# Shifting attention scores bank by bank in a fused attention and feed-forward kernel, with value products and the first unit's work re-slotted

## Chip, cores, metric

One Trainium2 chip, one core. The metric is device time in microseconds for one execution, as a median over runs.

TensorE, VectorE, ScalarE and GpSimd are called PE, DVE, ACT and POOL, as in the profile; PEld is PE's weight load. The clock in a profile is the share of PE's full clock that was granted.

## The reference

Pooled attention for 8 batches of 8 heads (sequence 576, head size 64; keys and values averaged over 8 rows, so 72 keys), then a feed-forward layer with a snake activation, all in float32:

```python
scores = scale * np.matmul(q, k_p.transpose(0, 1, 3, 2))        # (8, 8, 576, 72)
scores = scores - np.max(scores, axis=-1, keepdims=True)        # "the shift"
attn = np.exp(scores); attn = attn / (np.sum(attn, -1, keepdims=True) + 1e-09)
x = attention_output(attn, v_p)          # (4608, 512)
h = x @ w_in                             # (4608, 2048)
s = np.sin(alpha * h)
g = h + s * s / (alpha + 1e-09)
out = g @ w_out                          # (4608, 512)
```

## The kernel before

The hidden layer runs as nine units of 512 tokens. A unit is 28 slots, four groups of seven products (a Strassen scheme); a slot is four matmuls of 128x128x256, 1.73 us of PE. The attention for the next unit's tokens is slipped between slots. So unit 0 holds the attention of batch 1 (and the rest of batch 0), units 1 to 6 that of batches 2 to 7, and units 7 and 8 have none. The output layer follows.

A `slot` first runs what is left of the slot before, then the extra attention work, then its product:

```python
for slot in range(7 * self.NJ):
    J, k = divmod(slot, 7)
    for f in self.left: f()          # bank-to-bank copies and sines (ACT), sums (DVE)
    for f in extra[slot]: f()        # attention work
    ...                              # k == 0: b1 = bank(); left0: b6 = bank(); k == 1: b5 = bank(); left2: b7 = bank()
    product(p, ...)                  # p = (1, 5, 6, 2, 7, 3, 4)[k]
```

The kernel uses PSUM as eight banks. Banks 0 to 4 rotate (`bank()` takes the next), 5 to 7 serve attention. Scores come in pairs of tiles, two banks a tile: banks 5 and 6, and banks x and 7, where x is the rotating bank that the next group will take. A shift is two DVE instructions (maximum, subtract) over both banks at once:

```python
def two_scores(j):
    x = (self.turn + 1) % 5
    views = []
    for i, (c, d) in ((2 * j, (5, 6)), (2 * j + 1, (x, 7))):
        m = 6 if i == 3 else NP
        ps = self.PS[:, c:d + 1:d - c, 0:m * Sp].rearrange("p e (h k) -> p e h k", h=m)   # banks c and d
        ...                                                # score matmuls into ps
    for i, m, ps in views[::-1 if j else 1]:
        mx = self.sm.tile([P, 2, 6], F32, name="mx2")
        nc.vector.tensor_reduce(out=mx[:, :, 0:m], in_=ps, axis=AX, op=OP.max)
        nc.vector.tensor_tensor(out=E(i)..., in0=ps, in1=mx..., op=OP.subtract)
```

The products with the values use half or a quarter of PE's rows each. `halves` are products on 64 rows, `last_keys` on 32; `ordered` is a tiny DVE copy that keeps products on different rows apart when they write one bank (`rest`). Here hp = 0, 1 use rows 0-63 and hp = 2, 3 rows 64-127:

```python
halves(ps[2], main[2], True); halves(rest[:, 0], ...); halves(rest[:, 1], ...)
ordered()
for hp in (0, 1): halves(ps[hp], main[hp], True)
halves(rest[:, 2], ...); halves(rest[:, 3], ...)
halves(ps[3], main[3], True)
for hp in (0, 1): last_keys(rest[:, hp], more[hp])
ordered()
for hp in (0, 2, 1, 3): last_keys(ps[hp], main[hp])
for hp in (2, 3): last_keys(rest[:, hp], more[hp])
```

Of the kernel before, what the change touches and what calls it, by code (L numbers as in the profile page):

```python
# [13 lines left out]
F32 = mybir.dt.float32  # L14
AX = mybir.AxisListType.X
AF = mybir.ActivationFunctionType
OP = mybir.AluOpType
PSUM = bass.MemoryType.PSUM

P = 128  # L20
# [20 lines left out]
class Kernel:  # L41
    def __init__(self, tc, q, k, v, w_in, w_out, alpha, out):
        self.tc, self.nc = tc, tc.nc
        self.q, self.k, self.v = q, k, v
        self.w_in, self.w_out, self.alpha, self.out = w_in, w_out, alpha, out
        self.B, self.H, self.S, self.D = q.shape
        self.Sp = self.S // POOL
        self.DM = self.H * self.D
        self.FF = w_in.shape[1]
        self.K1 = self.DM // P  # L50
        self.K2 = self.FF // P
        self.NP = self.H // 2
        self.NU = self.B * self.S // (2 * TH)
        self.NJ = self.K2 // 2 // JW
        self.xT = {}
        self.T = self.S // 4

        self.gd = self.nc.dram_tensor("g_bridge", (2, self.NJ * JW, P, self.B * self.S), F32, kind="Internal").ap()
# [154 lines left out]
    def attention(self, b):  # L213
# [19 lines left out]
                nc.tensor.transpose(ps[:, j, :], kp[:, j].rearrange("p e d -> p (e d)"), self.ident[:NP * m, :NP * m])  # L233
            nc.vector.tensor_copy(out=kb[:].rearrange("p hp (x j) -> p j hp x", j=3), in_=ps.rearrange("p j (hp x) -> p j hp x", hp=NP))

        def q_t(i):

            n = rows[i]
            x = self.qm[b][:n].rearrange("p (t hp x) -> p t hp x", t=5, hp=NP)[:, i]
            if b not in self.qt:  # L240
                self.qt[b] = self.qt_view(self.qp.tile([P, 5 * H * D], F32, name="q"))
            ps = self.abank([P, NP, P])
            for hp in range(NP):
                nc.tensor.transpose(ps[:, hp, :n], x[:, hp], self.ident[:n, :n])
            nc.scalar.copy(out=self.qt_tiles(b)[:, i, :, :n], in_=ps[:, :, :n])

        def columns(hp, i):

            if b < 2:
                return [(c, self.qt_tiles(b)[:, i, hp, c:c + 64]) for c in range(0, rows[i], 64)]  # L250
            if i < 4:
                return [(64 * c, self.qt[b][:, i, hp, 2 * c:2 * c + 2].rearrange("p t i -> p (t i)")) for c in range(2)]
            return [(32 * a, self.qt[b][:, a, hp, 4]) for a in range(2)]

        def two_scores(j):

            x = (self.turn + 1) % 5
            views = []
            for i, (c, d) in ((2 * j, (5, 6)), (2 * j + 1, (x, 7))):
                m = 6 if i == 3 else NP  # L260
                ps = self.PS[:, c:d + 1:d - c, 0:m * Sp].rearrange("p e (h k) -> p e h k", h=m)
                views.append((i, m, ps))
                for t in (i, 4) if i == 3 else (i,):
                    for hp in range(NP):
                        r0, h = (64 * (hp // 2), NP + hp % 2) if t == 4 else (0, hp)
                        for r, q in columns(hp, t):
                            for e in range(2):
                                s = slice(64 * e, 64 * e + 64)
                                nc.tensor.matmul(ps[r0 + r:r0 + r + q.shape[-1], e, h, :], q[s], kb[s, hp, :], start=True, stop=True)  # L269
            for i, m, ps in views[::-1 if j else 1]:  # L270
                mx = self.sm.tile([P, 2, 6], F32, name="mx2")
                nc.vector.tensor_reduce(out=mx[:, :, 0:m], in_=ps, axis=AX, op=OP.max)  # L272
                nc.vector.tensor_tensor(out=E(i).rearrange("p (e h) k -> p e h k", e=2), in0=ps,  # L273
                                        in1=mx[:, :, 0:m].unsqueeze(3).to_broadcast([P, 2, m, Sp]), op=OP.subtract)

        def products(i):

# [226 lines left out]
        def all_values():  # L504

            hps = 0, 2, 1, 3
            ps = dict(zip(hps, (self.psum([P, 4 * P], i) for i in (5, 6, 7, (self.turn + 4) % 5))))
            rest = self.psum([P, 4, 64], (self.turn + 1) % 5)
            main, more = ({hp: value_parts(hp, r) for hp in hps} for r in (False, True))

            def halves(o, parts, start):
                for e, (w, x) in enumerate(parts[0]):
                    nc.tensor.matmul(o[64 * e:64 * e + 64], w, x, start=start, stop=False, skip_group_check=True)  # L513

            def last_keys(o, parts):
                w, x = parts[1]
                nc.tensor.matmul(o, w.rearrange("p e d -> p (e d)"), x, start=False, stop=True, skip_group_check=True)  # L517
            def ordered():
                nc.vector.tensor_copy(out=self.sm.tile([P, 1], F32, name="order")[:], in_=rest[:, 1, 0:1])
            halves(ps[2], main[2], True)  # L520
            halves(rest[:, 0], more[0], True)
            halves(rest[:, 1], more[1], False)
            ordered()
            for hp in (0, 1):
                halves(ps[hp], main[hp], True)
            halves(rest[:, 2], more[2], False)
            halves(rest[:, 3], more[3], False)
            halves(ps[3], main[3], True)
            for o, hp in ((rest[:, 0], 0), (rest[:, 1], 1)):
                last_keys(o, more[hp])  # L530
            ordered()
            for hp in hps:
                last_keys(ps[hp], main[hp])
            for hp in (2, 3):
                last_keys(rest[:, hp], more[hp])
            self.vp.pop(b)
            for hp in hps:
                to_x(ps[hp].rearrange("p (t j) -> p j t", t=4), hp, 0, 512)
            to_x(rest, slice(0, 4), 512, 64)

        return SimpleNamespace(**{f.__name__: f for f in (k_t, q_t, products, score, two_scores, exp, norm, new_a, turn, move, values, values_rest, all_values,
                                                          k_head, q_head, rest_q, products_head, soft_head, norm_head, norm_rest, a_head, a_rest)})


# [261 lines left out]
    def first_batch(self):  # L806

        nc = self.nc
# [44 lines left out]
                A.norm_head(hp - 1, nc.vector if hp == 1 else nc.gpsimd)  # L853
        self.load_q_rest(0, self.q_rest)
        self.load_q(1)
        self.load_w_in_part(1)
        for e in range(2):
            self.load_k(1, e)
        A.norm_head(3, nc.vector)
        self.sum_v_rows(0, 0, 2)  # L860
        A.a_head(0, (1, 7, 0))
# [8 lines left out]
    def carry(self, u):  # L870
# [5 lines left out]
        if u == 0:  # L876
            A0, A = self.att[:2]
            at(1, A0.values, (2, 3), (2, 7))
            at(1, self.sums_of_x, 0, 1)
            at(1, self.sums_of_x, 0, 2)  # L880
            at(1, self.sums_of_x, 0, 3)
            at(2, self.load_w_in_part, 2)
            at(2, self.load_w_in_part, 3)
            at(3, A0.rest_q)
            at(3, A0.score, 4)
            at(3, self.pairs_q, 1, (0, 1))
            at(4, self.pairs_q, 1, (2, 3, 4))
            at(5, self.combine_w_in, 1, (0, 1))
            at(6, self.combine_w_in, 1, (2, 3))
            at(6, A.k_t)  # L890
            at(7, self.load_v, 1, 0)
            at(7, self.load_v, 1, 1)
            for i in range(5):
                at((4, 5, 6, 7, 8)[i], A.q_t, i)
            for i in range(2):
                at((10, 12)[i], A.two_scores, i)
            for i in range(4):
                at((14, 15, 15, 15)[i], A.exp, i)
                at((15, 15, 16, 16)[i], A.norm, i)
                at((16, 16, 17, 17)[i], A.turn, i)  # L900
            at(10, self.combine_w_in, 2, (0, 1, 2, 3), self.nc.gpsimd)
            at(16, self.combine_w_in, 3, (0, 1, 2, 3), self.nc.gpsimd)
            at(15, A0.exp, 4)
            at(20, A0.norm_rest)
            at(23, A0.a_rest)
            at(24, lambda: A0.values_rest((5, 6, 7, (self.turn + 1) % 5)))
            at(17, A.new_a)
            at(17, A.move, 0)
            at(17, A.move, 1)
            at(25, A.all_values)  # L910
            at(9, self.load_q, 2)
            at(14, self.load_q, 3)
            for e in range(2):
                at(16, self.load_k, 2, e)
            at(26, self.att[2].k_t)
            turn = 23
        else:
            at(0, self.sums_of_x, u, 2)
            at(0, self.sums_of_x, u, 3)
        if 0 < u < last:  # L920
            A = self.att[b]
            for i in range(2):
                at((3, 5)[i], A.two_scores, i)
            for i in range(4):
                at((8, 9, 10, 10)[i], A.exp, i)
                at((9, 10, 11, 11)[i], A.norm, i)
                at((12, 12, 13, 13)[i], A.turn, i)
# [335 lines left out]
```

## Time and profile before

| | before |
|---|---|
| time, median (lowest to highest) | 975.57 us (972.2 to 980.65, 4 runs) |
| profiled span | 969.3 us |
| PE busy, whole span | 920.7 us, 95% |
| PE idle from slot 1 of unit 0 (27.9 us) to the value products of unit 6 | 37.5 us |
| time at half clock in that stretch | 23.9 us (seven windows of 3.41 us) |
| output stage | 368 us at full PE, not touched |

How to read it: PE is the bound, so the question is where PE stands still and where its clock is halved. The lines for that are in the prediction: shares, waits of PE, the sums by unit, and the chain of unit 1. (The chain is the work that ended last, followed back from each piece to what released it.) The numbers in `name <- name: 26.7, 10, 2.9` are microseconds in total, how many waits, and the longest. Lines of source are named L721 and so on; L269 is the score matmul, L272 and L273 the shift, L721 the products of the hidden layer, L700 and L788 DVE's sums, L513 and L517 the 64-row and 32-row value products.

### The profile page before, as it was taken

What the parts mean: (1) busy time and instruction counts of PE and PEld (TensorE: products, weight loads), DVE (VectorE), ACT (ScalarE), POOL (GpSimd) and SP (SyncE); (2) the same over time, 40 slices, a digit from 0 to 9 for tenths busy, and PEclk for the clock granted to TensorE, in tenths of its full rate; (3) what the DMA queues carried; (4) which work ended last, traced back from release to release, by engine and by line L of the source; (5) the groups of instructions that cost most, each with busy time, mean ns of one, the idle gap of its engine ahead of it and who ended that gap; (6) DMA issues with size and microseconds to landing.
All of it is one profiled execution on the core that took longest, in us unless ns stands there. A gap on an engine that the chain in (4) does not pass through costs nothing.

```text
span 969.3 us, 17586 instructions
## 1 busy us (share of the span) xinstructions
PE 920.7 (95%) x6953; PEld 828.6 (85%) x6953; DVE 667.7 (69%) x990; ACT 434.4 (45%) x995; POOL 154.1 (16%) x147
## 2 busy tenths in 40 slices
PE   7977899998997998989999999999999999999997
PEld 6766678886786876878888889999999999999997
DVE  6548574664645654647346688997979797979795
ACT  3745576674763864757688662111111111111111
POOL 4257151341412503412000000000000000000000
PEclk9999999999998998999999999999999999999999
DMA  9964656666565563661642724625253625252511
GB/s 245 229 190 119 177 154 174 196 166 185 148 175 164 142 173 99 173 191 58 225 170 87 234 88 122 203 75 172 74 172 74 172 74 172 77 171 75 173 23 37
DMA packets 134130, 141.12 MB, mean 146 GB/s; under 512 B 49808, under 2 KB 102048, under 8 KB 134048
## 3 DMA queue, kind: packets, MB, share of 16 engines
q1 hardware_dynamic: 132976, 138.81, 49.5%
q10 hardware_dynamic: 1072, 1.19, 0.4%
q8 instruction: 55, 0.90, 0.4%
q14 instruction: 27, 0.22, 0.1%
HBM read 75.37 MB, written 47.19 MB: 126 GB/s over the span
## 4 chain that ended last, share of the span: by engine, by line
PE 83%; DVE 7%; ACT 4%; issue 1%; POOL 0%; DMA 0%; SPq 0%; DVEq 0%; ACTq 0%
PE PS L1019 39%; PE PS L721 39%; PE PS L513 2%; DVE mx L272 2%; DVE ex L273 2%; ACT s L734 2%; DVE h L788 1%; PE PS L269 1%; PE PS L517 1%; DVE sm L305 1%; DVE h L700 1%; ACT s L727 1%; ACT PS L747 0%; ACT ex L299 0%; ACT p L761 0%
## 5 line engine op out<-in xcount | busy, mean ns | idle before, releaser
L721 PE MATMUL PS<-home,a 128*128 128x256 f32 x1152 | 274.8, 391 | 25.3 <-DVE ex L273 17.1
L721 PEld LDWEIGHTS PS<-home,a 128*128 128x128 f32 x1152 | 222.8, 196 | 62.7 <-DVE ex L273 18.0
L721 PE MATMUL PS<-home,as 128*128 128x256 f32 x864 | 203.2, 384 | 10.5 <-DVE ex L273 9.6
L721 PEld LDWEIGHTS PS<-home,as 128*128 128x128 f32 x864 | 163.4, 191 | 35.8 <-DVE ex L273 10.3
L1019 PE MATMUL PS<-s,wb 128*128 128x144 f32 x896 | 119.4, 286 | 0.4 <-ACT PS L1132 0.4
L700 DVE TENSOR_TENSOR h<-PS,p 128x512 f32<-128x512 f32 x72 | 49.2, 684 | 98.2 <-PE PS L721 56.6
L1019 PEld LDWEIGHTS PS<-s,wb 128*128 128x128 f32 x896 | 113.7, 190 | 0.7 <-ACT PS L1132 0.6
L734 ACT ACTIVATE s<-s,c 128x256 f32<-128x256 f32 (+1 forms) x216 | 110.0, 572 | 0.0
L117 POOL TENSOR_TENSOR kvin<-kvin 96x768 f32<-96x768 f32 (+3 forms) x42 | 70.1, 1669 | 205.1 <-DMA kvin<-in_v_dram 186.3
L727 ACT ACTIVATE s<-h,al 128x256 f32<-128x256 f32 x144 | 65.2, 501 | 78.1 <-DVE h L700 78.1
L727 ACT ACTIVATE s<-PS,al 128x256 f32<-128x256 f32 x144 | 60.0, 467 | 54.2 <-PE PS L721 42.4
L1132 ACT COPY PS<-PS 128x144 f32<-128x144 f32 x56 | 14.7, 263 | 146.0 <-PE PS L1019 144.6
L788 DVE TENSOR_TENSOR h<-PS,s 128x512 f32<-128x512 f32 x36 | 24.6, 684 | 73.1 <-ACT s L734 73.1
L1019 PE MATMUL PS<-r,wb 128*128 128x144 f32 x512 | 73.2, 286 | 0.0
L1019 PE MATMUL PS<-s,a 128*128 128x144 f32 x512 | 73.2, 286 | 0.0
L1019 PEld LDWEIGHTS PS<-r,wb 128*128 128x128 f32 x512 | 67.1, 190 | 0.1
L1019 PEld LDWEIGHTS PS<-s,a 128*128 128x128 f32 x512 | 67.0, 190 | 0.0
L1019 PE MATMUL PS<-s,we 128*128 128x144 f32 x384 | 54.9, 286 | 0.0
L1019 PE MATMUL PS<-x,wb 128*128 128x144 f32 x384 | 54.9, 286 | 0.0
L1151 ACT COPY PS<-PS 128x144 f32<-128x144 f32 x56 | 14.7, 263 | 88.2 <-PE PS L1019 88.2
L1019 PEld LDWEIGHTS PS<-s,we 128*128 128x128 f32 x384 | 50.4, 190 | 0.1
L1019 PEld LDWEIGHTS PS<-x,wb 128*128 128x128 f32 x384 | 50.3, 190 | 0.0
(176 smaller groups left out, 1175.4 us busy)
## 6 DMA issues: line engine op xcount, KB each, us to landing
g_bridge<-h SPq DMA_DIRECT2D x72, 512.0 KB
r<-g_bridge SPq DMA_DIRECT2D x31, 1152.0 KB
out_dram<-o SPq DMA_DIRECT2D x128, 72.0 KB
kvin<-in_k_dram SPq DMA_DIRECT2D x14, 576.0 KB
q<-in_q_dram SPq DMA_DIRECT2D x7, 1024.0 KB
kvin<-in_v_dram SPq DMA_DIRECT2D x14, 512.0 KB
aM<-tr SPq DMA_DIRECT2D x56, 92.0 KB
aM<-tr SPq DMA_DIRECT2D x56, 88.0 KB
```

Of the source, the lines that this page charges most:

```text
L117: self.nc.gpsimd.tensor_tensor(out=t[..., 0:w] if w > D else out, in0=t[..., 0:w], in1=t[..., w:2 * w], op=OP.add)
L272: nc.vector.tensor_reduce(out=mx[:, :, 0:m], in_=ps, axis=AX, op=OP.max)
L273: nc.vector.tensor_tensor(out=E(i).rearrange("p (e h) k -> p e h k", e=2), in0=ps, in1=mx[:, :, 0:m].unsqueeze(3).to_broadcast([P, 2, m, S ...
L513: nc.tensor.matmul(o[64 * e:64 * e + 64], w, x, start=start, stop=False, skip_group_check=True)
L700: add = lambda o, x, y: nc.vector.tensor_tensor(out=o, in0=x, in1=y, op=OP.add)
L721: nc.tensor.matmul(ps[:, jj, :], self.A[p][:, kk, f * P:(f + 1) * P], x[:, kk, :], start=(start and jj == 0 and kk == 0), stop=(kk == 1), ...
L727: nc.scalar.activation(out=G.s[:, i, jj, j, :], in_=src[:, jj], func=AF.Sin, scale=self.al[:, f:f + 1])
L734: nc.scalar.activation(out=x, in_=x, func=AF.Square, scale=self.c[:, f:f + 1])
L788: add = lambda o, x, y: self.nc.vector.tensor_tensor(out=o, in0=x, in1=y, op=OP.add)
L1019: nc.tensor.matmul(out, W[:, J // 2, J % 2, :], A[:, J, :], start=(start and J == 0), stop=(J == self.NJ - 1), skip_group_check=True)
L1132: nc.scalar.copy(out=x1[:, 0, :], in_=x0[:, 1, :])
L1151: nc.scalar.copy(out=x1[:, 1, :], in_=x1[:, 0, :])
```

## The change

The intent: take PE's waits for the shift away, spread DVE's work over more slots, place value products so that row halves alternate, and unbunch the attention work of unit 0. The diff, cut to its core:

```diff
-            for i, (c, d) in ((2 * j, (5, 6)), (2 * j + 1, (x, 7))):
+            for i, banks in ((2 * j, (x, 7)), (2 * j + 1, (5, 6))):
-                ps = self.PS[:, c:d + 1:d - c, 0:m * Sp].rearrange(...)
+                ps = [self.psum([P, m, Sp], c) for c in banks]
-            for i, m, ps in views[::-1 if j else 1]:   (both shifts at once)
+            for i, m, ps in tiles:
+                self.shifts.append(lambda i=i, m=m, ps=ps: shifts(i, m, ps))
+            two_shifts()
+            if j == 0:
+                two_shifts()
+        def shifts(i, m, ps):            # odd tiles: one view of banks 5:7; even tiles: bank by bank
+            if i % 2: ps, y = [self.PS[:, 5:7, 0:m * Sp]...], [y]
+            else:     y = y[:, 0], y[:, 1]
+            for z, o in zip(ps, y): (reduce max of z, then o = z - max)
 # value products
-            for hp in (0, 1):
+            for hp in (0, 3, 1):
                 halves(ps[hp], main[hp], True)
 ...
-            halves(ps[3], main[3], True)
-            last_keys of rest 0, 1
+            last_keys of ps[2], ps[3], then of rest 0, 1
             ordered()
-            last_keys of ps[0], ps[2], ps[1], ps[3]
+            last_keys of ps[0], ps[1]
             last_keys of rest 2, 3
 # units 1 to 6
+            at(6, A.two_shifts)          # the last shift, one slot after its scores (slot 5)
 # unit 0 (slots, before -> after)
 #   keys of batch 1 loaded before, not after, the second part of w_in
 #   rest_q 3 -> 2; k_t 6 -> 4; q_t 4,5,6,7,8 -> 4,4,7,8,9 (the first two copied by DVE, not ACT)
 #   pairs_q(2, 3, 4): slot 4 in both, but now behind q_t and k_t in program order
 #   two_scores 10, 12 -> 5, 10 with the last shift at 11; exp 14,15,15,15 -> 9,9,15,15
 #   norm 15,15,16,16 -> 10,10,16,16; turn 16,16,17,17 -> 13,13,17,17
 #   w_in sums of part 1: DVE, slots 5, 6 -> POOL, slot 4; of part 3: POOL, slot 16 -> 10
```

More of the change, by code (lines that the diff above doesn't have):

```diff
@@ L54, in __init__ @@
         self.NJ = self.K2 // 2 // JW
-        self.xT = {}
+        self.xT, self.shifts = {}, []
         self.T = self.S // 4
@@ L234, in k_t, with q_t @@
             nc.vector.tensor_copy(out=kb[:].rearrange("p hp (x j) -> p j hp x", j=3), in_=ps.rearrange("p j (hp x) -> p j hp x", hp=NP))
-        def q_t(i):
+        def q_t(i, copy=nc.scalar.copy):
             n = rows[i]
@@ L244, in q_t @@
                 nc.tensor.transpose(ps[:, hp, :n], x[:, hp], self.ident[:n, :n])
-            nc.scalar.copy(out=self.qt_tiles(b)[:, i, :, :n], in_=ps[:, :, :n])
+            copy(out=self.qt_tiles(b)[:, i, :, :n], in_=ps[:, :, :n])
         def columns(hp, i):
             if b < 2:
+                if i == 4:
+                    return [(0, self.qt_tiles(b)[:, 4, hp, 0:64])]
                 return [(c, self.qt_tiles(b)[:, i, hp, c:c + 64]) for c in range(0, rows[i], 64)]
@@ L257, in two_scores @@
             x = (self.turn + 1) % 5
-            views = []
-            for i, (c, d) in ((2 * j, (5, 6)), (2 * j + 1, (x, 7))):
+            tiles = []
+            for i, banks in ((2 * j, (x, 7)), (2 * j + 1, (5, 6))):
                 m = 6 if i == 3 else NP
-                ps = self.PS[:, c:d + 1:d - c, 0:m * Sp].rearrange("p e (h k) -> p e h k", h=m)
-                views.append((i, m, ps))
+                ps = [self.psum([P, m, Sp], c) for c in banks]
+                tiles.append((i, m, ps))
                 for t in (i, 4) if i == 3 else (i,):
@@ L268, in two_scores, with two_shifts @@
                                 s = slice(64 * e, 64 * e + 64)
-                                nc.tensor.matmul(ps[r0 + r:r0 + r + q.shape[-1], e, h, :], q[s], kb[s, hp, :], start=True, stop=True)
-            for i, m, ps in views[::-1 if j else 1]:
-                mx = self.sm.tile([P, 2, 6], F32, name="mx2")
-                nc.vector.tensor_reduce(out=mx[:, :, 0:m], in_=ps, axis=AX, op=OP.max)
-                nc.vector.tensor_tensor(out=E(i).rearrange("p (e h) k -> p e h k", e=2), in0=ps,
-                                        in1=mx[:, :, 0:m].unsqueeze(3).to_broadcast([P, 2, m, Sp]), op=OP.subtract)
+                                nc.tensor.matmul(ps[e][r0 + r:r0 + r + q.shape[-1], h, :], q[s], kb[s, hp, :], start=True, stop=True)
+            for i, m, ps in tiles:
[3 more added lines that the diff above has]
+                two_shifts()
+        def two_shifts():
+            self.shifts.pop(0)()
+        def shifts(i, m, ps):
+            y = E(i).rearrange("p (e h) k -> p e h k", e=2)
+            if i % 2:
+                ps, y = [self.PS[:, 5:7, 0:m * Sp].rearrange("p e (h k) -> p e h k", h=m)], [y]
+            else:
+                y = y[:, 0], y[:, 1]
+            for z, o in zip(ps, y):
+                w = list(z.shape)[:-1]
+                mx = self.sm.tile([P, 12], F32, name="mx2")[:, 0:m * (1 + i % 2)]
+                if i % 2:
+                    mx = mx.rearrange("p (e h) -> p e h", e=2)
+                nc.vector.tensor_reduce(out=mx, in_=z, axis=AX, op=OP.max)
+                nc.vector.tensor_tensor(out=o, in0=z, in1=mx.unsqueeze(len(w)).to_broadcast(w + [Sp]), op=OP.subtract)
         def products(i):
@@ L527, in all_values @@
             halves(rest[:, 3], more[3], False)
-            halves(ps[3], main[3], True)
-            for o, hp in ((rest[:, 0], 0), (rest[:, 1], 1)):
-                last_keys(o, more[hp])
+            for hp in (2, 3):
+                last_keys(ps[hp], main[hp])
+            for hp in (0, 1):
+                last_keys(rest[:, hp], more[hp])
             ordered()
-            for hp in hps:
+            for hp in (0, 1):
                 last_keys(ps[hp], main[hp])
@@ L539, in all_values @@
             to_x(rest, slice(0, 4), 512, 64)
-        return SimpleNamespace(**{f.__name__: f for f in (k_t, q_t, products, score, two_scores, exp, norm, new_a, turn, move, values, values_rest, all_values,
+        return SimpleNamespace(**{f.__name__: f for f in (k_t, q_t, products, score, two_scores, two_shifts, exp, norm, new_a, turn, move, values, values_rest, all_values,
                                                           k_head, q_head, rest_q, products_head, soft_head, norm_head, norm_rest, a_head, a_rest)})
@@ L855, in first_batch @@
         self.load_q(1)
-        self.load_w_in_part(1)
         for e in range(2):
             self.load_k(1, e)
+        self.load_w_in_part(1)
         A.norm_head(3, nc.vector)
@@ L883, in carry @@
             at(2, self.load_w_in_part, 3)
-            at(3, A0.rest_q)
+            at(2, A0.rest_q)
             at(3, A0.score, 4)
             at(3, self.pairs_q, 1, (0, 1))
+            at(4, self.combine_w_in, 1, (0, 1, 2, 3), self.nc.gpsimd)
+            at(4, A.q_t, 0, self.nc.vector.tensor_copy)
+            at(4, A.q_t, 1, self.nc.vector.tensor_copy)
+            at(4, A.k_t)
             at(4, self.pairs_q, 1, (2, 3, 4))
-            at(5, self.combine_w_in, 1, (0, 1))
-            at(6, self.combine_w_in, 1, (2, 3))
-            at(6, A.k_t)
             at(7, self.load_v, 1, 0)
             at(7, self.load_v, 1, 1)
-            for i in range(5):
-                at((4, 5, 6, 7, 8)[i], A.q_t, i)
             for i in range(2):
-                at((10, 12)[i], A.two_scores, i)
+                at((5, 10)[i], A.two_scores, i)
+            at(11, A.two_shifts)
+            for i in range(2, 5):
+                at(5 + i, A.q_t, i)
+            at(9, A0.exp, 4)
             for i in range(4):
-                at((14, 15, 15, 15)[i], A.exp, i)
-                at((15, 15, 16, 16)[i], A.norm, i)
-                at((16, 16, 17, 17)[i], A.turn, i)
+                at((9, 9, 15, 15)[i], A.exp, i)
+                at((10, 10, 16, 16)[i], A.norm, i)
+                at((13, 13, 17, 17)[i], A.turn, i)
             at(10, self.combine_w_in, 2, (0, 1, 2, 3), self.nc.gpsimd)
-            at(16, self.combine_w_in, 3, (0, 1, 2, 3), self.nc.gpsimd)
-            at(15, A0.exp, 4)
+            at(10, self.combine_w_in, 3, (0, 1, 2, 3), self.nc.gpsimd)
             at(20, A0.norm_rest)
```

## The prediction

> **What bounds the kernel now.** I read the page first: engine shares, then the chain that ended last.
>
> ```profile
> PE 920.7 (95%) x6953; PEld 828.6 (85%) x6953; DVE 667.7 (69%) x990; ACT 434.4 (45%) x995; POOL 154.1 (16%) x147
> PE 83%; DVE 7%; ACT 4%; issue 1%; POOL 0%; DMA 0%; SPq 0%; DVEq 0%; ACTq 0%
> ```
>
> TensorE is the bound: removing work elsewhere helps only where TensorE waits for it. The second line holds 11% of DVE and ACT, so such places exist. The waits of TensorE say which:
>
> ```profile
> PE PS L721 <- DVE ex L273: 26.7, 10, 2.9
> PE PS L721 <- DVE h L700: 5.9, 7, 4.7
> ```
>
> Ten waits, 26.7 us, for L273, the subtraction of the score maximum. The busy sums by stage (length, PE, PEld, DVE, ACT and POOL busy, granted clock, DMA) place them. The rows are unit 0 (attention of batch 1) and units 1 to 6, each without its value products:
>
> ```profile
> 40.00:96.00 56.00, 45.54 (x353) 37.18 (x352) 35.49 (x54) 32.78 (x69) 31.03 (x27) 0.94 0.54 150
> 104.00:158.40 54.40, 50.43 (x380) 42.66 (x380) 33.97 (x55) 34.94 (x71) 19.04 (x17) 1.00 0.59 165
> 165.00:216.70 51.70, 50.67 (x381) 42.94 (x383) 34.48 (x55) 35.25 (x72) 19.07 (x17) 1.00 0.64 177
> 223.00:280.60 57.60, 52.13 (x383) 44.32 (x381) 33.99 (x55) 35.59 (x72) 19.03 (x17) 0.97 0.57 160
> 287.00:346.20 59.20, 53.72 (x384) 45.50 (x384) 34.89 (x56) 35.51 (x72) 19.04 (x17) 0.94 0.56 155
> 353.00:411.40 58.40, 52.93 (x379) 44.82 (x382) 34.84 (x56) 35.02 (x70) 19.02 (x17) 0.94 0.49 135
> 418.00:472.50 54.50, 50.55 (x380) 42.77 (x378) 31.76 (x53) 35.08 (x71) 11.42 (x11) 1.00 0.44 123
> 525.00:573.80 48.80, 48.80 (x229) 42.96 (x228) 37.75 (x57) 31.76 (x68) 0.00 (x0) 1.00 0.47 159
> 590.00:958.00 368.00, 368.00 (x3006) 368.00 (x3005) 317.26 (x416) 64.22 (x205) 0.00 (x0) 1.00 0.40 115
> ```
>
> Length less PE busy is idle: 10.5, 4.0, 1.0, 5.5, 5.5, 5.5, 4.0 us, 36 us in all. The granted clock adds a cost: (1 - clock) x length is 3.4 + 1.7 + 3.6 + 3.5 = 12.2 us. The last two rows (a unit without attention, and the output stage) have nothing to win, and the change leaves them alone.
>
> Unit 2, with the same work, idles only 1.0 us. The code says why. The second score tile of a pair is read as one strided view of banks x and 7, x being the next free of five rotating banks. Each unit takes 16 banks, so x moves by one: 1 in unit 0, then 3, 4, 0, 1, 2, 3. If the framework takes the view as everything from x to 7, it orders the shift against products into the banks between, which hold no scores. With x = 4 nothing lies between but 5 and 6. By x the predicted waits are 2, 1, 0, 2, 2, 2, 1: ten, as counted. The built program agrees: in unit 1 the product after the first scores waits for DVE before the change and for nothing after.
>
> What such a wait is made of stands in the chain of unit 1 (start, us, what):
>
> ```profile
> 109.58 2.05 ACT s L734 x4
> 111.66 1.82 DVE h L788 x2
> 113.48 0.68 DVE mx L272
> 114.18 0.76 DVE ex L273
> 114.94 0.68 DVE mx L272
> 115.64 0.77 DVE ex L273
> 116.45 3.72 PE PS L721 x16
> ```
>
> The shifts queue behind ACT's squares and DVE's sums; scores ended at 113.6, products restart at 116.45.
>
> **What the Trainium skill says.** "PSUM — Partial Sum Buffer", PSUM bank collisions: engines must be kept apart on the same bank and quadrant; so reading 7 and x needs no order against a product in another bank. The trace cannot show this; the code and the list of waits do. "TensorE: Matmul & The Clock Gate", Part 1: the clock halves after an idle window of about 3.4 us of a free-running 3413 ns grid. The trace agrees: the clock is 0.55 in 365 to 372 us, right after a 2.9 us wait, yet 1.00 after the same wait in unit 1. "TensorEngine Tiling (Array Packing)", Key Properties and Gotcha 1: row tiles run in parallel, but must not write one bank together. The value products agree: products on rows 0-63 and 64-127 overlap in the trace, and each unit has two small DVE copies that keep them apart. "ScalarE: Activation LUTs", What ACT_TABLE_LOAD costs: about 1283 ns a load; the trace has 1.28 us.
>
> **Part 1, views by bank, units 1 to 6.** Even tiles now take (x, 7) and are shifted bank by bank; odd tiles take (5, 6) in one view. DVE cost: a reduce and subtract of 576 elements take 0.75 and 0.76 us; of 288 (L290, L291) 0.45 and 0.45. So an even tile costs 1.8 instead of 1.5 us, 0.6 us a unit, off the path with DVE under 65% busy. What remains true: at slot 5 the second pair overwrites 5 and 6. In unit 1's times the shifts end at 113.4 + 1.8 + 1.5 = 116.7; TensorE, no longer held, does two slots of 1.73 us from 113.6 and reaches those banks at about 117.6. No wait, by 0.9 us. The last shift moves to slot 6, behind the sums that free banks, so L700 runs at once instead of 2 us late, and ACT's copies come earlier.
>
> A later wait stays: norms in slots 9 to 11, then the L700 sum, then the product of slot 13. I put the sum's end at 133.2 against 132.6 for TensorE, so 0.6 us. From the scores to slot 13 unit 1 would take 20.8 us. Before, the six units took 25.1, 22.0, 27.9, 29.4, 29.0, 25.0. Gains 4.3, 1.2, 7.1, 8.6, 8.2, 4.2: 33.6 us, about 8.5 of it clock. I book 31, since six copies of a slack of 0.9 us may not all hold.
>
> **Part 2, value products.** Before, TensorE takes 2.6 to 3.1 us for L513, since the fourth 64-row product is issued after a small one that waits for DVE's copy. Placing it between two on the other rows starts it about 0.9 us sooner. I count 0.6 us x 7 = 4, and book 3.5.
>
> **Part 3, unit 0.** The query transposes of the rest move up a slot: the 1.1 us wait for their copy goes. Two score waits (2.8 and 2.3 us) go, with one half-clock window (1.7). Exps, norms and turns, bunched in slots 14 to 17, made a 4.7 us wait followed by another half-clock window; half of them now come at slots 9 to 13. Keys load ahead of the second weight part (1 MB at about 270 GB/s, 3.8 us sooner), and its sums move from DVE to POOL, 5.1 us. New costs: ACT switches tables twice more (2.6 us), and I expect TensorE to wait 1.3 us for its copy at slot 11 and 0.9 at slot 18. POOL does 10 us of weight sums before the later norms, so these end near 72 and the sum for slot 20 near 74: a wait of about 2 us. Slot 20 starts at 84.5 before, so 10 us earlier; the wait of 1.2 us for the last norms at slot 23 takes about what half-clock took before. I book 9.5.
>
> **Sum.** 31 + 3.5 + 9.5 = 44 us. The profiled run took 971.06 us: 927. The median of 975.9 probably holds more half-clock, which the change mostly removes, so I take 926.
>
> **Rivals.** (a) A true wait takes the false one's place: at slot 5 TensorE waits for shifts of banks 5 and 6. For it: DVE's shifts start only when the squares are done, and slack is 0.9 us. Against: two slots of products lie between. At 1.5 us a unit it costs 9: 935. (b) Unit 0 only shifts its stall: POOL's queue or ACT's tables hold slots 11 to 20, and a gap brings the half clock. For: POOL is full from 49 to 72 us by my count. It would leave 3 of the 9.5 us: 933. (c) DVE or DMA becomes the bound: DVE is at 34.9 of 59 us a unit and DMA at 0.6; neither fits. (d) The waits were hidden anyway, the time going to the next wait: the slot-13 chain speaks for it; then only the clock and unit 0 gain, about 950. Unit 2, which lacks the waits and is 3 to 8 us shorter, speaks against.
>
> **Range and chances.** All well, with no residual waits: 917. With (a) and (b) together: 942. So 917 to 941. Over 2% faster is below 956.4, which needs more than half the gain lost: 0.96 faster, 0.03 same, 0.01 slower.
>
> **What would show it.** After: TensorE's waits for the subtraction fall from 26.7 to under 3 us; idle in each of units 1 to 6 is about 1 us and their lengths agree within 1 us whatever x is; the clock is 1.00 in all of them; L513 takes about 2 us a unit; unit 0's value products start near 86 instead of 96.7 us; the output stage stays 368 us. It is wrong if the shift's waits reappear before the scores of slot 5, if half-clock windows persist in units 3 to 5, or if unit 0 ends less than 5 us earlier.

## The result, and the profile after

The changed kernel takes 932.78 us (930.97 to 937.39, 4 runs) against 975.57 us: a ratio of 0.9564, interval 0.9509 to 0.962. It lies in the range, 6.8 us above the predicted time. Ratios here are the mean time of one kernel's runs over that of the other's in the same rounds, so they are not quite the ratio of the medians that are quoted. Executions over 1.5% slower than the fastest of the same kernel are left out of the means. All outputs are right.

Line numbers move: L743 are now the hidden products, L271 the scores, L294 and L295 the shift, L722 and L810 DVE's sums, L534 and L538 the value products, L614 the weight sums, L328 the norms on POOL. First the page after, its engine shares and the shares of the chain that ended last:

```profile
PE 910.0 (98%) x6953; PEld 825.0 (89%) x6953; DVE 672.0 (72%) x1016; ACT 436.3 (47%) x995; POOL 160.2 (17%) x151
PE 90%; DVE 4%; ACT 2%; POOL 2%; issue 1%; DMA 0%; SPq 0%; POOLq 0%; DVEq 0%; ACTq 0%
```

DVE does more (26 more instructions, 4 us), and yet its share of the chain falls from 7 to 4%. The waits of PE after:

```profile
PE PS L743 <- DVE h L722: 3.4, 8, 2.1
PE PS L271 <- DVE kblk L234: 3.1, 1, 3.1
PE PS L271 <- issue: 2.7, 2, 1.5
```

No wait for the subtraction is left, out of ten and 26.7 us. Two lines are new, and the prediction had neither. The sums by stage after, in the columns of the prediction (unit 0, units 1 to 6, output):

```profile
40.00:91.50 51.50, 46.06 (x355) 37.48 (x353) 32.54 (x57) 34.74 (x70) 32.63 (x28) 0.93 0.64 172
98.30:148.40 50.10, 49.91 (x378) 42.75 (x376) 33.73 (x59) 35.01 (x70) 19.04 (x17) 1.00 0.65 182
154.50:206.80 52.30, 50.66 (x379) 43.31 (x377) 35.12 (x59) 35.21 (x71) 19.03 (x17) 1.00 0.63 177
212.90:263.50 50.60, 50.41 (x380) 43.25 (x377) 34.13 (x59) 35.24 (x71) 19.04 (x17) 1.00 0.65 182
269.70:322.00 52.30, 50.88 (x383) 43.53 (x381) 35.29 (x60) 35.32 (x72) 19.03 (x17) 1.00 0.64 178
328.10:378.70 50.60, 50.41 (x379) 43.23 (x377) 36.13 (x60) 35.22 (x71) 19.04 (x17) 1.00 0.57 157
384.80:435.50 50.70, 50.51 (x384) 43.31 (x382) 32.47 (x57) 35.25 (x71) 11.43 (x11) 1.00 0.47 134
552.80:920.70 367.90, 367.90 (x3006) 367.90 (x3005) 317.20 (x416) 64.22 (x205) 0.00 (x0) 1.00 0.40 115
```

Units 1, 3, 5 and 6 idle 0.2 us each, where they idled 4.0 to 5.5. The clock is 1.00 in all six. Units 2 and 4 are 1.7 us longer than their neighbours: most of that is the "issue" line, 1.46 and 1.23 us. Unit 0 still runs at 0.93. The output stage is as it was.

Unit 1 in the timeline of PE (start, length, what, and in brackets the idle time before it), to be set against the chain of unit 1 in the prediction:

```profile
106.64 1.33 PE L271 MATMUL PS<-kblk,q 64*64 64x72 f32 x64
107.90 3.72 PE L743 MATMUL PS<-home,a 128*128 128x256 f32 x16
111.55 1.67 PE L271 MATMUL PS<-kblk,q 64*64 64x72 f32 x96
...
127.47 3.72 PE L743 MATMUL PS<-home,a 128*128 128x256 f32 x16 [0.19 <-DVE h L722]
```

The products follow the first scores at once (before: 2.87 us later), the second scores find their banks free, and the one wait left is the one forecast at slot 13, 0.19 us. From the first scores to slot 13 it is 20.8 us.

Where the 37.3 us of the two profiled spans (969.3 and 932.0) went, by the start of the value products of each unit:

| stretch | before | after | gain |
|---|---|---|---|
| start to PE's wait in slot 1 of unit 0 | 27.9 | 28.0 | -0.2 |
| rest of unit 0 (to its value products) | 68.8 | 63.5 | 5.3 |
| units 1 to 6 (six periods) | 375.8 | 344.0 | 31.8 |
| to the end | 496.8 | 496.5 | 0.3 |

### The profile page after: what moved, and what is told of

It is laid out like the page before. It is cut to its first block, busy times and chain, and to the rows that moved or that the text cites. A ratio compares the mean times of both kernels' runs of the same rounds, so it can differ in the third digit from the quotient of the medians.

```text
span 932.0 us, 17618 instructions
## 1 busy us (share of the span) xinstructions
PE 910.0 (98%) x6953; PEld 825.0 (89%) x6953; DVE 672.0 (72%) x1016; ACT 436.3 (47%) x995; POOL 160.2 (17%) x151
## 4 chain that ended last, share of the span: by engine, by line
PE 90%; DVE 4%; ACT 2%; POOL 2%; issue 1%; DMA 0%; SPq 0%; POOLq 0%; DVEq 0%; ACTq 0%
PE PS L743 42%; PE PS L1044 41%; PE PS L271 2%; PE PS L534 2%; PE PS L538 2%; DVE sm L326 1%; POOL as L614 1%; POOL ex L328 1%; DVE h L722 0%; ACT ex L320 0%; PE PS L839 0%; POOL a L614 0%; ACT p L783 0%; ACT PS L781 0%; DMA s<-in_moe_alpha_dram 0%
## 5 line engine op out<-in xcount | busy, mean ns | idle before, releaser
L743 PE MATMUL PS<-home,a 128*128 128x256 f32 x1152 | 267.1, 383 | 3.5 <-DVE h L722 3.4
L743 PEld LDWEIGHTS PS<-home,a 128*128 128x128 f32 x1152 | 217.4, 191 | 37.9 <-DVE h L722 6.6
L743 PE MATMUL PS<-home,as 128*128 128x256 f32 x864 | 201.5, 383 | 1.0 <-DVE home L716 1.0
L743 PEld LDWEIGHTS PS<-home,as 128*128 128x128 f32 x864 | 163.6, 191 | 24.4 <-DVE home L716 1.1
L722 DVE TENSOR_TENSOR h<-PS,p 128x512 f32<-128x512 f32 x72 | 49.1, 684 | 75.5 <-PE PS L743 47.2
L810 DVE TENSOR_TENSOR h<-PS,s 128x512 f32<-128x512 f32 x36 | 24.7, 685 | 65.0 <-ACT s L756 65.0
```

Source lines behind the costliest of these rows:

```text
L722: add = lambda o, x, y: nc.vector.tensor_tensor(out=o, in0=x, in1=y, op=OP.add)
L743: nc.tensor.matmul(ps[:, jj, :], self.A[p][:, kk, f * P:(f + 1) * P], x[:, kk, :], start=(start and jj == 0 and kk == 0), stop=(kk == 1), ...
L810: add = lambda o, x, y: self.nc.vector.tensor_tensor(out=o, in0=x, in1=y, op=OP.add)
```

## The experiments

Each kernel ran beside the kernel before, whose median was 974.2 to 976.6 us. Where a profile tells more than the median, it is used; unit 0 and the start vary by some microseconds from run to run (the wait in slot 1 comes at 26.7 to 31.3 us in the profiles), so small differences there need both.

| kernel | median us | ratio to before |
|---|---|---|
| changed | 932.78 | 0.9564 |
| before, views changed only | 943.40 | 0.9675 |
| changed, view undone | 957.32 | 0.9829 |
| changed, unit 0 undone | 933.24 | 0.9582 |
| changed, value order undone | 937.69 | 0.9605 |
| changed, last shift not spread | 935.70 | 0.9606 |
| changed, pairing copies earlier | 930.50 | 0.9554 |
| changed, weight sums later | 929.85 | 0.9559 |
| the last two together | 927.93 | 0.9529 |
| ... and 16 tiny matmuls | 926.88 | 0.9525 |
| ... and 32 instead | 931.37 | 0.9575 |
| 16, and half of the value order undone | 928.69 | 0.9523 |
| changed, again | 933.24 | 0.9551 |

### Is it the view, or the new order and spread?

Theory A: the strided view over banks x and 7 makes the framework order products behind shifts that they share no bank with. Rival B: the swap of bank pairs and the spreading of shifts bring the gain. One kernel is the kernel before with the view alone changed:

```diff
+                if i % 2:
+                    for e, c in enumerate((x, 7)):     # bank by bank
+                        z = self.psum([P, m, Sp], c); (reduce, subtract of z)
+                    continue
                 (banks 5 and 6: one view, as before)
```

> The kernel before with one edit: the tile in banks x and 7 is shifted bank by bank; same banks, same slots, same order. Theory A (the strided view made the framework order products behind shifts of other banks): TensorE's waits for the subtraction fall from 26.7 us in ten to under 3 us, units 1 to 6 are about 30 us shorter together with the half clock gone from units 3 to 5, time about 944 us, ratio 0.967. Rival B (the gain of units 1 to 6 comes from swapping the bank pairs and spreading the shifts over slots): the waits stay above 20 us and the time stays over 965 us.

Measured: 943.40 us, ratio 0.9675. The waits of PE in its profile:

```profile
PE PS L728 <- DVE h L707: 5.8, 7, 4.7
PE PS L728 <- ACT PS L754: 5.4, 7, 2.5
PE PS L728 <- ACT PS L766: 4.1, 7, 0.6
```

No wait for the subtraction is left here either, and no half-clock window in units 1 to 6. Theory A stands, at the size expected (944). The other kernel takes the view back in the changed kernel:

```diff
-            if i % 2: one view of banks 5:7;  else: bank by bank
+            c, d = (5, 6) if i % 2 else (x, 7)
+            ps, y = [self.PS[:, c:d + 1:d - c, 0:m * Sp]...], [y]
```

> The changed kernel with one edit taken back: the tile in banks x and 7 is again shifted in one strided view; swapped pairs, spread shifts, new unit 0 and value order stay. Theory A: waits for the subtraction come back, depending on x, in units with x other than 4, 15 to 30 us in all, with half-clock windows; time 955 to 968 us. Rival B: time stays within 3 us of the changed kernel's 932.8 us.

Measured: 957.32 us, 24.5 us above the changed kernel. The waits are back:

```profile
PE PS L741 <- DVE ex L293: 18.9, 10, 3.3
```

By unit there are 2, 1, 0, 2, 2, 2, 1, which is what x = 1, 3, 4, 0, 1, 2, 3 asks for; PE has three half-clock windows in units 3, 5 and 6, and one more right after the value products of unit 0. Each wait is shorter than before (1.7 and 1.8 us in most units instead of 2.9 and 2.4); that the tile in x and 7 is now shifted first would explain it. So rival B falls as the main cause, and A is shown from both sides: alone it gives three quarters of the gain.

### Is the spread worth something?

```diff
             two_shifts()
-            if j == 0:
-                two_shifts()
+            two_shifts()
-            at(6, A.two_shifts)      and the same in unit 0 at slot 11
```

> The changed kernel with the last shift of each batch (tile 3) done in the slot of its scores again instead of one slot later. Theory: DVE then does 2.1 us of shift ahead of the sums of slot 6, ACT's copies come later, and TensorE waits about 1.1 us in each of units 1 to 6 for ACT (as in the kernel with only the views changed, 0.48 + 0.60 us a unit): about 6 to 7 us more, 939 us. Rival (only the views matter, the spread is hidden): within 2 us of 932.8.

Measured: 935.70 us, 2.9 above, and units 1, 3 and 5 take 57.29 instead of 56.74 us each: 0.55 us a unit, half of what was expected. So the spread is real but smaller. The kernel with only the views changed takes 58.4 us in such units. Of its 1.67 us over the changed kernel, 0.24 are the value products (below) and 0.55 the spread. The remaining 0.88 is put down to the swap of the pairs, by which DVE now begins with the tile whose scores come first. That share was not run by itself. The edit also takes the spread out of unit 0: there the wait at slot 20 grows from 2.08 to 3.98 us, with two half-clock windows from 79.1 us on instead of one.

### Value products

```diff
-            for hp in (0, 3, 1): ...     (the whole of the new order)
+            for hp in (0, 1): ...        (the whole of the old order)
```

> The changed kernel with the order of the value products taken back. The 64-row value products should take 2.7 instead of 2.16 us in each of seven units: 3.8 us in all, so about 936.5 us. Rival: TensorE's time there is made up later by a shorter wait at slot 13 (0.2 us a unit is all that is left), so at most 1.3 us of it is hidden and the time is 2.5 us up at least.

Measured: 937.69 us, 4.9 above. But its runs span 934.06 to 943.08, and its profile has two more half-clock windows in the start and unit 0, which the edit cannot make. The steady units tell the size: 56.98 instead of 56.74 us, 0.24 us a unit, not 0.55. So "2.5 us up at least" is not what the edit shows by itself. The timelines of PE say where the rest stays. Before (unit 2), 64-row and 32-row products:

```profile
216.63 2.71 PE L513 MATMUL PS<-aM,vm 64*64 64x512 f32 x32
219.27 1.79 PE L517 MATMUL PS<-aM,vz 32*128 32x64 f32 x16
```

After (unit 2):

```profile
206.81 2.18 PE L534 MATMUL PS<-aM,vm 64*64 64x512 f32 x32
208.92 2.08 PE L538 MATMUL PS<-aM,vz 32*128 32x512 f32 x16
```

The 64-row part takes 2.11 us to the start of the next instead of 2.64; the 32-row part takes 2.00 us to the start of the hidden products instead of 1.72. Net, 0.24 us: the same as the steady units show. In the new order only two large products lie between the small ones that DVE's copy reads and the small ones that wait for it. PE's weight loads show it (unit 2 after):

```profile
210.34 0.52 PEld L538 LDWEIGHTS PS<-aM,vz 32*128 32x128 f32 x4 [0.67 <-DVE order L540]
```

So one half of the reorder pays and the other costs. If so, the new `halves` with the old `last_keys` is best. This was run on top of the best kernel at that point (16 tiny matmuls, below):

```diff
-            last_keys of ps[2], ps[3]; rest 0, 1; ordered(); ps[0], ps[1]; rest 2, 3
+            last_keys of rest 0, 1; ordered(); ps[0], ps[2], ps[1], ps[3]; rest 2, 3
```

> The kernel with both unit 0 edits and 16 tiny matmuls, and with half of the value reorder taken back: the 64-row products keep the new order, the 32-row products (last keys) go back to the old one, in which the two small ones come first and DVE's second ordering copy hides behind four large ones. Theory: the change won 0.55 us a unit in the 64-row part and lost about 0.3 in the 32-row part (1.72 to about 2.05 us), where TensorE's weight loads now wait 0.7 us for that copy. So values take about 3.9 instead of 4.12 us, units without a stop 56.5 instead of 56.74 us, about 1.7 us in all: 925.2 us. Rival: the 32-row part is slower because it starts earlier relative to DVE and ACT, whatever its order: units stay at 56.7 us.

Its timeline (unit 2):

```profile
210.84 2.18 PE L534 MATMUL PS<-aM,vm 64*64 64x512 f32 x32
212.95 1.79 PE L538 MATMUL PS<-aM,vz 32*128 32x64 f32 x16
```

2.11 + 1.72 us, and units without a stop take 56.45 instead of 56.74 us, as expected. The rival (later work, whatever the order) falls. The median, 928.69 us, missed the 925.2, and one run took 937.23: its time was lost in the start and unit 0 (see "weight sums" below). Against the changed kernel in the same rounds (a comparison of all these edits together, not of the value order),

> The changed kernel itself once more, on the same chip and in the same rounds as the kernel with all edits, so that the two can be compared without a change of chip: 931 to 934 us, and the stops in units 2 and 4 at the same places as in its first profile.

which took 933.24 us with its stops in units 2 and 4 as before, it is 4.5 us faster by the medians. Five of its six runs (927.11 to 929.92) lie below all five of the other (931.30 to 933.81). The intervals of the two ratios still touch.

### Unit 0: are the new slots worth anything?

The edit, cut to its core:

```diff
-            rest_q 2; k_t 4; q_t 4,4 (DVE), 7,8,9; two_scores 5, 10, two_shifts 11; exp 9,9,15,15; norm 10,10,16,16; turn 13,13,17,17
+            rest_q 3; k_t 6; q_t 4,5,6,7,8 (ACT); two_scores 10, 12, two_shifts 13; exp 14,15,15,15; norm 15,15,16,16; turn 16,16,17,17
             (weight sums and loads of keys as before, too)
```

> The changed kernel with unit 0's slots, its copies on ACT and the order of its loads taken back. If unit 0's new slots are worth what the profiles show (value products of unit 0 start at 91.5 instead of 96.7 us), the time is 3 to 5 us above the changed kernel's. But the old slots also lose their two false score waits by the new views (5.1 us and a half-clock window of 1.7), so the rival says that the new slots are worth nothing or less than nothing: time equal to or up to 3 us below the changed kernel's. Units 1 to 6 as in the changed kernel in both.

Measured: 933.24 us, the same as the changed kernel. So the unbunching gains nothing that the medians can tell: the old slots with the new views lose the score waits too, and keep the 1.1 us and 4.7 us waits. In the profiles the stretch from PE's wait in slot 1 to the value products takes 64.9 us here and 64.3 us with only the views changed, against 63.5 after and 68.8 before: most of what unit 0 gained came from the views. The new slots trade the old waits for others. Three are visible in the profile after.

First, the key block at slot 5. DVE's timeline, with idle time before in brackets:

```profile
42.52 1.29 DVE L245 COPY q<-PS 128x512 f32<-128x512 f32 x2 [3.86 <-ACT q L93]
43.72 0.53 DVE L234 COPY kblk<-PS 128x288 f32<-128x288 f32 x1
```

The key transposes had left PE at 39.5 us. But DVE's queue had two query copies in front; they write the buffer that ACT's pairing copies (L93) still read, and ACT did three of those behind its sines, until 42.5. PE's scores waited 3.06 us, and a half-clock window followed (45.8 to 49.2 us). Second, the norms of tiles 2 and 3 on POOL:

```profile
73.22 1.28 POOL L614 TENSOR_TENSOR as<-a,as 128x512 f32<-128x512 f32 x1
74.45 2.74 POOL L328 TENSOR_TENSOR ex<-ex,sm 128x576 f32<-128x576 f32 x2
```

They stand behind 11 us of weight sums (from 63.4 us on); their transposes hold DVE's sum, and PE waits 2.1 us at slot 20, with another half-clock window from 79.9 us. Two edits, one for each:

```diff
-            at(3, self.pairs_q, 1, (0, 1))
-            at(4, self.pairs_q, 1, (2, 3, 4))
+            at(3, self.pairs_q, 1, (0, 1, 2, 3, 4))
```

> The changed kernel with one edit in unit 0: ACT's pairing copies of query tiles 2 to 4 move from slot 4 to slot 3, ahead of ACT's sines. Theory: DVE's first query copy of slot 4 writes the buffer that these pairing copies read, waits 3.9 us for them, and holds up the key block behind it, so TensorE waits 3.1 us at slot 5 with a half-clock window after it. Then that wait falls below 1 us, the half-clock window near 46 us goes, and the time is 3 to 5 us less: 928 to 930 us. Rival (the key block is late because of its own data from POOL): the wait stays near 3 us and so does the time.

Measured: 930.50 us. The 3.06 us wait and the window after it are gone from the profile, so the cause is settled; in the profile unit 0 is 4.4 us shorter (59.0 against 63.5 us), as expected. The medians differ by 2.3 us only, with runs from 926.94 to 932.86. The norms on POOL still hold slot 20 for 2.06 us.

```diff
-            at(10, self.combine_w_in, 3, (0, 1, 2, 3), self.nc.gpsimd)
+            at(16, self.combine_w_in, 3, (0, 1, 2, 3), self.nc.gpsimd)
```

> The changed kernel with one edit in unit 0: the weight sums of the fourth part go to POOL at slot 16 behind the norms, as before the change, instead of at slot 10. Theory: these 5 us on POOL hold the two later norms; without them TensorE's 2.1 us wait at slot 20 goes, with the half-clock window after it (1.7 us): 929 to 931 us. Rival (DVE or ACT would be late anyway): the wait stays above 1 us.

Measured: 929.85 us. In its profile the norms start at 70.6 us, the wait at slot 20 is 1.0 us instead of 2.1, and there is no half-clock window from 30 us to the output. The wait is halved, not gone: the chain before it now runs over ACT (a table load and exps, 67.4 to 69.4 us), DVE's sums and POOL's norms, so the rival is right for the other half. That the window after the key block is missing here is not this edit's doing: the wait there was 2.46 us, and in the changed kernel run again a window followed 2.48 us. Both edits:

> Both edits of unit 0 together. If they are independent: 925 to 927 us, no TensorE wait over 1 us and no half-clock window between 30 us and the output stage, so unit 0's value products start 6 to 8 us sooner. If they share one bottleneck: no better than the better of the two.

Measured: 927.93 us (927.04 to 928.29), all runs below all of the changed kernel's, ratio 0.9529. Unit 0 from PE's wait in slot 1 to the value products takes 57.6 us in the profile, against 63.5 after and 68.8 before. The forecast of 925 to 927 was missed by a microsecond, and two waits of a microsecond or more remain: 1.8 us for the keys at slot 4 and 1.0 at slot 20. So it is two bottlenecks, mostly independent.

Third, key sums on POOL (and in the slowest run below the weight sums too) now run beside DVE's own sums. DVE after, sums of two operands in SBUF, 128x512 (before, the same instruction took 0.68 to 0.69 us each time):

```profile
34.67 2.29 DVE L716 TENSOR_TENSOR home<-home,home 128x512 f32<-128x512 f32 x1
```

The keys landed 4.3 us sooner (POOL starts on them at 29.7 instead of 34.0 us), as intended; so POOL's sums fell on DVE's, and PE waited 0.97 us for them. The Trainium skill, "GPSIMD Engine Reference", Specifications, says that POOL shares its SBUF interfaces with DVE, in contention where DVE has two SBUF inputs. The trace agrees: after, 47 such sums of DVE with none of POOL's beside them took 0.68 to 0.69 us each, and the five with one took 0.68 to 2.30. The new order of loads is not needed for it: with unit 0 undone, in a profile whose start was 3 us longer, the sums met too and PE waited 0.57 us. In the slowest run of the kernel with the value order mixed (937.23 us, profiled) six of DVE's sums from 32.6 to 43.5 us took 1.5 to 2.3 us each, all beside POOL's, PE waited 4.58 us and ran at half clock for 6.8 us. That is where the spread of these kernels' runs can come from. No edit was run that moves only this, so its share is not measured.

### The stops inside the scores of units 2 and 4

The "issue" line: in every profile of a kernel with the new score order and no extra matmuls, PE stops in the second scores of unit 2, and in all but one (the view undone) in unit 4 as well, with no semaphore behind it. After (unit 2):

```profile
168.29 0.98 PE L271 MATMUL PS<-kblk,q 64*64 64x72 f32 x48
170.73 0.92 PE L271 MATMUL PS<-kblk,q 64*64 64x72 f32 x48 [1.46 <-issue]
```

The trace lists the DMA that fetches instructions. On one queue a 16,384-byte fetch comes for every 256 PE instructions on average, so I take it for PE's. One begins at 168.03 us, just before these scores, and lists 1.25 us; the stop ends at 170.73. Between it and the fetch before lie 447 PE instructions, where 200 to 300 is usual; but 415 lie before the fetch at 60.68 us, where PE doesn't stop. The second scores take 192 instructions in 1.6 us, the products 16 in 1.73 us. The Trainium skill, "Runtime: NRT & Kernel Launch", Instruction fetch mechanics, says that instructions are refilled in 16 KiB blocks of 256 and that the cost of a block boundary is mostly hidden. The size and the count agree with the trace; the hiding fails here. The kept traces say more than the intervals do. In the 13 profiles other than the one before the change there are 26 such stops of over 0.15 us (one of them with the old score order). Counted over all of PE's recorded instructions, weight loads and the sequencer's included, every one falls at 193 above a multiple of 256, whether 0, 64 or 128 instructions were put ahead, and each ends 2.6 to 3.0 us after a fetch of 16,384 bytes began. The test shifts the stream by a fraction of a block:

```diff
+            at(4, lambda: [self.nc.tensor.matmul(self.psum([32, 1], (self.turn + 1) % 5), self.ident[:32, :32],
+                           self.ident[:32, 0:1], start=True, stop=True) for _ in range(16)])     # or 32
             at(4, A.k_t)
```

> The kernel with both unit 0 edits, plus 16 tiny matmuls (32x32 weights, one column, never read) in unit 0 while TensorE waits for the keys: 64 more entries of TensorE's instruction stream, no other change. Every profile of a kernel with the new score order shows TensorE stop inside the scores of units 2 and 4 for 0.5 to 1.6 us with no semaphore behind it, where over 400 instructions lie between two 16 KB fetches of its instruction queue, against some 250 elsewhere. Theory (the stop is a wait for instructions, and its place is set by where the stream's blocks of 256 fall): shifted by a quarter block, the stops in units 2 and 4 leave or shrink and may show in other units, 926 to 928 us. Rival (the stop belongs to something those units do, such as a load at that time): both stops stay as they are, time 927.9 us plus the time of the tiny matmuls.

> The same with 32 tiny matmuls, 128 entries, half a block. Theory: the stops of units 2 and 4 are gone, or are at other units; if none takes their place the time is about 2 us less, 925.5 to 926.5 us. Rival: both stops stay in units 2 and 4.

Measured: 926.88 and 931.37 us. With 16, units 2 and 4 have no stop (56.74 us each), and unit 3 gets one of 0.92 us. PE in units 2 and 3 of that kernel:

```profile
162.13 1.67 PE L271 MATMUL PS<-kblk,q 64*64 64x72 f32 x96
...
221.40 0.44 PE L271 MATMUL PS<-kblk,q 64*32 64x72 f32 x11 [0.92 <-issue]
```

With 32, units 2 and 4 are free too, and stops come in unit 0 (0.81 us), 3 (1.10) and 5 (0.30). So the stop's place goes with the position in the instruction stream, at one place in every 256, and the rival falls. That the missing thing is the fetch rests on the trace's fetches, not on a run that changes the fetch alone. 32 is slower than none by 3.4 us in the medians, though its stops add up to less (2.2 us against 2.5); its profile shows one more wait, of 0.6 us, and the rest stays open.

### The best version

The kernels with both unit 0 edits run at 926.9 to 928.7 us in three forms that the medians do not separate. The simplest, both edits alone, takes 927.93 us: ratio 0.9529, 4.9 us below the changed kernel by the medians. The last form, with the value order mixed, has the shortest steady unit (56.45 us).

## Why the prediction was right, and where its sizes were off

- **The false order by the strided view: right.** The count by x (2, 1, 0, 2, 2, 2, 1) holds in the kernel that takes the view back, the waits vanish in the one that changes it alone, and the clock rises to 1.00 in units 1 to 6.
- **Rival (a), a true wait at slot 5: wrong.** No unit waits there for a shift. The slack held in all six; in unit 2, for example, the shift of banks 5 and 6 ended at 167.63 us, and the second scores began at 168.29.
- **The wait at slot 13: right, with a smaller size.** 0.19 us instead of 0.6; the 20.8 us from scores to slot 13 are as worked out.
- **Units 1 to 6: 31 us booked.** They gain 31.8 us; 1.9 of these are value products (26.9 to 25.0 us, six times), so the part is worth 29.9. Against it stand the two stops, 2.7 us, for which the prediction had no step.
- **Value products: 0.6 us a unit counted, 3.5 us booked, 2.1 found** (31.2 to 29.1 us over seven units; 0.24 us in a steady one). The 64-row part won about what was said (2.64 to 2.11 us). The mis-sized term is the 32-row part, which was not worked out at all: it lost 0.28 us to the wait for DVE's copy.
- **Unit 0: 9.5 us booked, 5.3 found.** Slot 20 waits 2.1 us as forecast; the waits forecast at slots 11, 18 and 23 (1.3, 0.9 and 1.2 us) did not come, and slot 13 waits 0.18 us. The step that failed is the list of new costs set against the removed waits ("Two score waits go"): it left out DVE's query copies at slot 4. They wait for ACT's pairing copies: 3.06 us of wait and a half-clock window, shown by the edit that removes them. And "half of them now come at slots 9 to 13" is worth nothing measurable against the old slots under the new views. POOL's sums beside DVE's, which the list lacked too, made 0.97 us of wait. The value products of unit 0 start at 91.5 us instead of the 86 forecast: 5.2 us earlier, just clear of the prediction's own sign of being wrong ("less than 5 us earlier").
- **The sum: 44 us forecast (31 + 3.5 + 9.5), 37.3 found in the profiles (29.9 + 2.1 + 5.3).** The 6.7 us between are 4.2 from unit 0, 1.4 from the value products and 1.1 from units 1 to 6, where the stops of 2.7 us outweigh better sizes elsewhere. For the stops, too, the lengths of units 1 to 6 do not agree within 1 us as forecast.
- **Rival (b), unit 0 only shifts its stall: right in kind.** It was given 933, with another mechanism (POOL and ACT tables) leading; the largest new wait was the buffer. That 932.8 us was measured is chance: unit 0 kept 5.3 us of its gain, not the 3 of this rival, and the rest was lost elsewhere.
- **The reading of the clock: too firm.** The prediction says that the trace agrees with a window of about 3.4 us. The wait that it names is 2.86 us long (362.57 to 365.43), shorter than that, and half clock began at 364.5 us, before the wait was over. See the list at the end.

## What to carry to other kernels

Write a read of two far banks as two reads, when the framework behaves as if it tracked a strided view by its extent: count the waits against the positions in between, and the pattern gives it away. When work is moved earlier to unbunch it, check for each moved instruction whose buffer it writes and what stands before it in the queue of its engine; here a copy that looked ready waited 3.9 us for readers that had been left behind in another queue. A wait of two or three microseconds on PE can cost 1.7 us more by the clock (half of a 3.41 us window), so count both, and look for stops without a semaphore where many short matmuls follow each other.

## What the Trainium skill lacked or had wrong

- "Runtime: NRT & Kernel Launch", Instruction fetch mechanics: block boundaries are said to be mostly hidden. Bursts of short score matmuls (96 records) stopped PE for 0.3 to 1.6 us where a block's fetch fell just before or in them, until 2.6 to 3.0 us after the fetch began, and 64 more instructions ahead moved the stop to another unit. The page gives no figure for such a stop.
- "TensorE: Matmul & The Clock Gate", Part 1: half clock is said to follow an idle window of about 3.4 us. Here windows of 3.41 us at 0.50 followed waits of 2.1 to 3.1 us, shorter than a window (for example 3.06 us of wait until 44.31 and 0.50 from 45.8 to 49.2), and not every such wait: 2.87 us in unit 1 before had none. In the changed kernel run again, a window began at 94.4 us with no wait over 0.53 us in the 10 us before it.
- "ScalarE: Activation LUTs", What ACT_TABLE_LOAD costs: the load's 1283 ns agree, but the page adds a drain of about 1380 ns to each switch. In unit 1 before, ACT's work ends at 130.40 us, the load runs from 130.42 us for 1.28 and the exp starts at 131.71; no drain shows.
